# A hedgehog-attention + FFN layer on one core: the attention tiles rewritten and laid between the FFN matmuls in a fixed order

## The chip, the cores and the metric

The kernel runs on one core of a Trainium2 chip. The metric is the device time of one execution in microseconds (us), and lower is better. "Span" is the time from the first to the last instruction in the trace; the device time is about 2 us longer.

Engines are named as in the profile: PE (TensorE matmuls), PEld (PE's weight loads, which overlap its matmuls), DVE (VectorE), ACT (ScalarE), POOL (GpSimd), SP (SyncE, here a DMA queue). PSUM is the memory that PE writes to; DVE and ACT copy results out of it ("evict").

"Tile" below means 128 of the 2048 tokens, so there are 16 tiles.

## The reference

```
x: 2048 x 640, H = 32 heads of 20, F = 1728
q, k, v  = layernorm(x) @ wqkv                      # LayerNorm 1
pq, pk   = per head: q @ w_phi, k @ w_phi           # 20 x 20 each
phi_q    = [softmax(pq), softmax(-pq)]  (40 features), phi_k the same
kv, z    = sum over tokens of phi_k^T v, phi_k      # per head, needs ALL tokens
o        = (phi_q @ kv) / (phi_q . z + 1e-6)
h        = x + o @ wo
out      = h + silu(layernorm(h) @ w1) @ w2         # LayerNorm 2, FFN
```

The state kv needs every token's keys. So all keys come first (the key stage), and the queries and the FFN of a tile can follow at any time after that.

## The kernel before

It has four stages, one after another: LayerNorm 1 and folding `w_phi` into the projection weights; the key stage; the query stage for all 16 tiles; the FFN in four groups of four tiles. A tool orders the instructions of each engine. These are the parts that the change touches, with cuts marked:

```python
def p1_stage_AB(t):                       # key stage, tile t
    psv = ...; psk = ...                  # V and K projections, columns split 512 + 128
    ...
    nc.scalar.activation(Ek4[:, :, 0, 0:DH], psk3, AF.Exp, scale=1.0)
    nc.scalar.activation(Ek4[:, :, 1, 0:DH], psk3, AF.Exp, scale=-1.0)
    nc.vector.tensor_reduce(Sk[:], Ekb[:, :, 0:DH], axis=AX.X, op=ALU.add)   # L258
    nc.vector.reciprocal(Sk[:], Sk[:])                                       # L259
    nc.vector.tensor_tensor(Ekb..., Ekb..., Sk broadcast, op=ALU.mult)       # L260
...
def p2_stage_A/N(t): ...                  # query: projection, exp, and the same three
                                          # DVE operations again (L369 to L371)
def p2_stage_C1/C2(t): ...                # 16 transposes of Eq, evicted by ACT
def p2_stage_E(t): ...                    # output = numerator / denominator (DVE)
def p2_stage_G(t): ...                    # o @ wo, and x added by matmuls with the identity
def ln2_tile(t, pool): ...                # LayerNorm 2: bn_stats etc. on DVE
...
def ffn_q(q):
    for fc in range(FC):
        rows = P if fc < FC - 1 else 64   # 1728 = 13 x 128 + 64
        ...                               # first product, 5 matmuls of 512 columns
        nc.scalar.activation(sg[0:rows, :], psh[0:rows, :], AF.Sigmoid)
        nc.vector.tensor_tensor(shT[0:rows, fc, :], psh[0:rows, :], sg[0:rows, :], op=ALU.mult)
    for si in range(4):
        for n0, n1 in ((0, 512), (512, 640)):
            for fc in range(FC):
                rows = P if fc < FC - 1 else 64
                nc.tensor.matmul(psy[:, n0:n1], shT[0:rows, fc, ...], w2_sb[0:rows, fc, n0:n1], ...)
```

The softmax here doesn't subtract the row's maximum and nothing guards it: scores larger than these inputs give would overflow.

Of the kernel before, what the change touches and what calls it, by code (L numbers as in the profile page):

```python
# [10 lines left out]
AX = mybir.AxisListType  # L11

BF16 = mybir.dt.bfloat16
F32 = mybir.dt.float32


@with_exitstack
def kernel(
# [11 lines left out]
    nc = tc.nc  # L30
# [3 lines left out]
    S = T * P  # L34
# [5 lines left out]
    FC = 14  # L40
    EPS = 1e-5

    x_t = A_x.rearrange("b (t p) d -> p (b t) d", p=P)
    out_t = out.rearrange("b (t p) d -> p (b t) d", p=P)

    persist = ctx.enter_context(tc.tile_pool(name="persist", bufs=1))
    early = ctx.enter_context(ExitStack())
    lnp = early.enter_context(tc.tile_pool(name="ln1", bufs=1))
    fp_ = early.enter_context(tc.tile_pool(name="fold", bufs=1))
    fps = early.enter_context(tc.tile_pool(name="foldps", bufs=2, space=bass.MemoryType.PSUM))  # L50
    lns = early.enter_context(tc.tile_pool(name="ln1s", bufs=3))
    lnps = early.enter_context(tc.tile_pool(name="ln1ps", bufs=2, space=bass.MemoryType.PSUM))
# [3 lines left out]
    eps_t = persist.tile([P, 1], F32, name="eps_t")  # L56
    nc.gpsimd.memset(eps_t[:], EPS)
    nhalf_t = persist.tile([P, 1], F32, name="nhalf_t")
    nc.gpsimd.memset(nhalf_t[:], -0.5)

    wqkv_sb = fp_.tile([P, C, 3 * D], BF16, name="wqkv_sb")
    wqkv_v = A_wqkv.rearrange("(c p) n -> p c n", p=P)
    nc.sync.dma_start(wqkv_sb[:, :, 1 * D : 2 * D], wqkv_v[:, :, 1 * D : 2 * D])
    WPH = fp_.tile([DH, H, DH], BF16, name="WPH")
    nc.scalar.dma_start(WPH[:], A_w_phi.rearrange("h d f -> d h f"))
    X_sb = lnp.tile([P, T, D], BF16, name="X_sb")
    for g4 in range(4):
        nc.gpsimd.dma_start(
            X_sb[:, 4 * g4 : 4 * (g4 + 1), :], x_t[:, 4 * g4 : 4 * (g4 + 1), :]
        )  # L70
    for i in (2, 0):
        nc.sync.dma_start(wqkv_sb[:, :, i * D : (i + 1) * D], wqkv_v[:, :, i * D : (i + 1) * D])
    wo_sb = persist.tile([P, C, D], BF16, name="wo_sb")
    nc.sync.dma_start(wo_sb[:], A_wo.rearrange("(c p) n -> p c n", p=P))
    XT = persist.tile([P, C, S], BF16, name="XT")
    for c in range(C):
        nc.sync.dma_start_transpose(XT[:, c, :], A_x[0, :, c * P : (c + 1) * P])

    SID = fp_.tile([DH, 3 * P], BF16, name="SID")
    nc.gpsimd.memset(SID[:], 0.0)  # L80
    nc.vector.tensor_copy(SID[:, P : P + DH], ident[0:DH, 0:DH])
    phi_sb = fp_.tile([P, C, D], BF16, name="phi_sb")
    for r in range(C):
        pphi = fps.tile([P, H, 32], F32, name="psw")
        heads = []
        for h in range(H):
            r0 = DH * h
            if r0 // P != r and (r0 + DH - 1) // P != r:
                continue
            p0 = r0 - r * P  # L90
            heads.append((h, p0))
        for (h, p0) in heads:
            nc.tensor.matmul(
                pphi[:, h, 0:DH],
                SID[:, P - p0 : 2 * P - p0],
                WPH[:, h, :],
                start=True,
                stop=True,
            )
        h_lo = heads[0][0]  # L100
        h_hi = heads[-1][0] + 1
        if h_lo > 0:
            nc.gpsimd.memset(phi_sb[:, r, 0 : DH * h_lo], 0.0)
        if h_hi < H:
            nc.gpsimd.memset(phi_sb[:, r, DH * h_hi : D], 0.0)
        nc.scalar.copy(
            phi_sb[:, r, DH * h_lo : DH * h_hi].rearrange("p (h f) -> p h f", f=DH),
            pphi[:, h_lo:h_hi, 0:DH],
        )

    Wfq = persist.tile([P, C, D], BF16, name="Wfq")
    Wfk = persist.tile([P, C, D], BF16, name="Wfk")
    Wv = persist.tile([P, C, D], BF16, name="Wv")
    XnT = persist.tile([P, C, S], BF16, name="XnT")

    nc.vector.tensor_copy(Wv[:], wqkv_sb[:, :, 2 * D : 3 * D])

    WTs = {}
    for which in (1, 0):
        base = which * D  # L120
        WT = fp_.tile([P, C, D], BF16, name=f"WT{which}")
        for r in range(C):
            pwt = fps.tile([P, C, P], BF16, name="pwt")
            for ce in range(C):
                nc.tensor.transpose(  # L125
                    pwt[:, ce, :],
                    wqkv_sb[:, ce, base + r * P : base + (r + 1) * P],
                    ident[:],
                )
            nc.scalar.copy(WT[:, r, :], pwt[:].rearrange("p a b -> p (a b)"))  # L130
        WTs[which] = WT

    Xn = lnp.tile([P, T, D], BF16, name="Xn")

    def ln1_group(g):
        for tt in range(8):
            t = g * 8 + tt
            stats = lns.tile([P, 2, 6], F32, name="st1")
            for i in range(2):
                nc.vector.bn_stats(stats[:, i, :], X_sb[:, t, i * 320 : (i + 1) * 320])  # L140
            mv = lns.tile([P, 2], F32, name="mv1")
            nc.vector.bn_aggr(mv[:], stats[:])
            rstd = lns.tile([P, 1], F32, name="rstd1")
            nc.vector.tensor_scalar_add(rstd[:], mv[:, 1:2], EPS)
            nc.gpsimd.tensor_tensor(rstd[:], rstd[:], nhalf_t[:], op=ALU.pow)
            nmr = lns.tile([P, 1], F32, name="nmr1")
            nc.vector.tensor_scalar(
                out=nmr[:], in0=mv[:, 0:1], scalar1=rstd[:, 0:1], scalar2=-1.0,
                op0=ALU.mult, op1=ALU.mult,
            )  # L150
            nc.vector.tensor_scalar(
                out=Xn[:, t, :], in0=X_sb[:, t, :],
                scalar1=rstd[:, 0:1], scalar2=nmr[:, 0:1],
                op0=ALU.mult, op1=ALU.add,
            )
        for c in range(C):
            pst = lnps.tile([P, 8, P], BF16, name="pXT")
            for tt in range(8):
                t = g * 8 + tt
                nc.tensor.transpose(pst[:, tt, :], Xn[:, t, c * P : (c + 1) * P], ident[:])  # L160
            if g == 0:
                nc.vector.tensor_copy(
                    XnT[:, c, g * 8 * P : (g + 1) * 8 * P],
                    pst[:].rearrange("p a b -> p (a b)"),
                )
            else:
                nc.scalar.copy(
                    XnT[:, c, g * 8 * P : (g + 1) * 8 * P],
                    pst[:].rearrange("p a b -> p (a b)"),
                )  # L170

    def fold(which):
        Wf = Wfk if which == 1 else Wfq
        WT = WTs[which]
        for ce in range(C):
            psw = fps.tile([P, D], F32, name="psw")
            for n0, n1 in ((0, 512), (512, 640)):
                for r in range(C):
                    nc.tensor.matmul(  # L179
                        psw[:, n0:n1],  # L180
                        WT[:, r, ce * P : (ce + 1) * P],
                        phi_sb[:, r, n0:n1],
                        start=(r == 0),
                        stop=(r == C - 1),
                    )
            if which == 1:
                nc.scalar.copy(Wf[:, ce, :], psw[:])
            else:
                nc.vector.tensor_copy(Wf[:, ce, :], psw[:])  # L189

    ln1_group(0)
    fold(1)
    fold(0)
    ln1_group(1)
    early.close()

    wpool = ctx.enter_context(tc.tile_pool(name="wpool", bufs=1))
    w1_sb = wpool.tile([P, C, F], BF16, name="w1_sb")
    nc.sync.dma_start(w1_sb[:], B_w1.rearrange("(c p) n -> p c n", p=P))
    w2_sb = wpool.tile([P, FC, D], BF16, name="w2_sb")  # L200
    nc.sync.dma_start(
        w2_sb[:, 0:13, :], B_w2[0 : 13 * P].rearrange("(c p) n -> p c n", p=P)
    )
    nc.sync.dma_start(w2_sb[0:64, 13, :], B_w2[13 * P : F, :])
    HnT = wpool.tile([P, C, S], BF16, name="HnT")

    KVBD = persist.tile([P, 16, 42], BF16, name="KVBD")
    nc.vector.memset(KVBD[:], 0.0)
    p2pre_ctx = ctx.enter_context(ExitStack())
    p2pre = p2pre_ctx.enter_context(tc.tile_pool(name="p2pre", bufs=1))  # L210
    p1ctx = ctx.enter_context(ExitStack())
# [10 lines left out]
    def p1_stage_AB(t):  # L222
# [11 lines left out]
        for n0, n1 in ((0, 512), (512, 640)):  # L234
# [29 lines left out]
            op=ALU.mult,  # L264
        )
        ek_state[t] = Ek
        vp_state[t] = Vp

    def p1_stage_C(t):
        Ek = ek_state[t]  # L270
# [364 lines left out]
```

## Time and profile before

| | before |
|---|---|
| device time, median | 351.51 us (350.58 to 352.51, 4 runs) |
| span of the profiled run | 350.2 us |
| what limits, by stage | DVE from 56 to 211 us, PE from 211 us on |

These are lines of the profile page of the kernel before: busy time of each engine with its share of the span, then the shares of the chain of work that ended last, by engine.

```profile
PE 301.1 (86%) x2597; PEld 171.2 (49%) x2642; DVE 235.3 (67%) x407; ACT 164.9 (47%) x239; POOL 62.0 (18%) x101
...
PE 49%; DVE 33%; ACT 6%; DMA 4%; POOL 4%; issue 3%; SPq 0%; DVEq 0%; POOLq 0%; ACTq 0%
```

The averages say little: PE 86%, DVE 67%. The windows view of the kernel before tells more. Each row is a stretch of time, its length, the busy us of each engine in it (with the number of instructions), the clock granted to PE as a share of full speed, the DMA share and GB/s. The stretches are load and folding, key stage, query stage, FFN.

```profile
core 0: us, PE busy (x) PEld busy (x) DVE busy (x) ACT busy (x) POOL busy (x), PEclk, DMA share, GB/s
0.00:56.00 56.00, 38.85 (x320) 24.18 (x326) 39.84 (x115) 19.89 (x32) 23.01 (x48) 1.00 0.57 153
56.00:115.00 59.00, 52.27 (x577) 30.95 (x585) 54.79 (x49) 37.01 (x55) 17.32 (x26) 1.00 0.22 77
115.00:211.00 96.00, 78.10 (x958) 53.85 (x972) 86.92 (x167) 68.40 (x91) 21.11 (x26) 0.96 0.01 1
211.00:350.00 139.00, 131.84 (x746) 62.25 (x760) 53.70 (x78) 39.64 (x63) 0.55 (x1) 1.00 0.06 20
```

In the query stage DVE is busy for 86.9 of 96 us; in the FFN PE is busy for 131.8 of 139 us while DVE is busy for 53.7. Two different engines limit two stages, and in each stage the other engine has time to spare.

Next, from the timeline of the kernel before, DVE alone, a stretch of the key stage: start, duration, operation.

```profile
68.42 1.49 DVE L260 TENSOR_TENSOR Ek<-Ek,Sk 128x1280 bf16<-128x1280 bf16 x1
69.82 1.48 DVE L258 TENSOR_REDUCE Sk<-Ek 128x64 f32<-128x1280 bf16 x1
71.34 0.55 DVE L259 RECIPROCAL Sk<-Sk 128x64 f32<-128x64 f32 x1
72.00 1.49 DVE L260 TENSOR_TENSOR Ek<-Ek,Sk 128x1280 bf16<-128x1280 bf16 x1
```

From one multiply to the next is 3.58 us, with no idle time between: this stage runs at DVE's pace.

The last extract is from the timeline of the kernel before, weight loads alone, in the second FFN product.

```profile
270.61 0.09 PEld L587 LDWEIGHTS <-shT 64*128 64x128 bf16 x1 [0.42 <-issue]
270.93 3.48 PEld L587 LDWEIGHTS <-shT 128*128 128x128 bf16 x27 [0.23 <-issue]
274.83 0.09 PEld L587 LDWEIGHTS <-shT 64*128 64x128 bf16 x1 [0.42 <-issue]
275.15 3.48 PEld L587 LDWEIGHTS <-shT 128*128 128x128 bf16 x27 [0.23 <-issue]
```

The load of the 64-row chunk takes no longer than the others (0.09 us), but there is a gap before it (0.42 us) and after it (0.23 us).

### The profile page before, as it was taken

To read this page: it belongs to the slowest core of one execution; us is meant where nothing else is said; L and a number is where in the kernel's file an instruction comes from. 1 tells how busy PE (TensorE), PEld (TensorE's weight loads), DVE (VectorE), ACT (ScalarE), POOL (GpSimd) and SP (SyncE) were. 2 spreads that over 40 slices of the span, in tenths; PEclk is the share of its full clock that TensorE was granted. 3 is DMA by queue.
4 is the path that set the end of the run, shared out by engine and by line. 5 is a ranking of instruction groups with operands and counts; after the bars stand their busy time and mean duration, and the time that the engine had idled before them with its cause. 6 is when DMAs were issued, how large, how long until landed. Compare 5 with 4: busy or idle time off the path is not lost.

```text
span 350.2 us, 6321 instructions
## 1 busy us (share of the span) xinstructions
PE 301.1 (86%) x2597; PEld 171.2 (49%) x2642; DVE 235.3 (67%) x407; ACT 164.9 (47%) x239; POOL 62.0 (18%) x101
## 2 busy tenths in 40 slices
PE   2299878999996779788999667999999999999995
PEld 2156445555553556455665543445544544444443
DVE  0985987999999999998989865441453145315421
ACT  3253049646466567867899455420742044104400
POOL 7430552333320012342231010000000000000000
PEclk9999999999999989999999899999999999999999
DMA  7995003910000000000000000001000100010011
GB/s 274 400 196 108 2 1 83 392 35 2 2 0 2 3 0 2 2 0 2 3 2 1 2 0 2 0 20 38 19 2 19 39 19 1 21 38 18 2 37 37
DMA packets 18997, 15.98 MB, mean 46 GB/s; under 512 B 11482, under 2 KB 17818, under 8 KB 18970
## 3 DMA queue, kind: packets, MB, share of 16 engines
q1 hardware_dynamic: 17744, 12.95, 12.8%
q0 software_dynamic: 576, 2.62, 1.8%
q8 instruction: 20, 0.33, 0.4%
q10 hardware_dynamic: 650, 0.03, 0.1%
q14 instruction: 7, 0.06, 0.0%
HBM read 10.35 MB, written 2.62 MB: 37 GB/s over the span
## 4 chain that ended last, share of the span: by engine, by line
PE 49%; DVE 33%; ACT 6%; DMA 4%; POOL 4%; issue 3%; SPq 0%; DVEq 0%; POOLq 0%; ACTq 0%
PE psy L587 19%; PE psh L569 16%; DVE Ek L260 6%; DVE Sk L258 6%; DMA wqkv_sb<-in_A_wqkv_dram 4%; PE psw L179 4%; DVE Sq L369 4%; PE psa L442 3%; DVE O L419 2%; DVE Sk L259 2%; DVE Eq L371 2%; DVE st L485 2%; POOL rstd L490 2%; PE psq L349 2%; PE psT L395 1%
## 5 line engine op out<-in xcount | busy, mean ns | idle before, releaser
L587 PE MATMUL psy<-w_sb,shT 128*128 128x128 bf16 (+3 forms) x441 | 72.4, 299 | 0.7 <-issue 0.5
L569 PE MATMUL psh<-HnT,w_sb 128*128 128x512 bf16 (+1 forms) x272 | 66.7, 379 | 2.9 <-DVE shT L578 1.7
L578 DVE TENSOR_TENSOR shT<-psh,sg 128x512 bf16<-128x512 f32 (+1 forms) x56 | 38.6, 691 | 38.3 <-ACT sg L577 38.3
L577 ACT ACTIVATE sg<-psh 128x512 bf16<-128x512 f32 (+1 forms) x56 | 33.3, 596 | 65.7 <-PE psh L569 61.4
L587 PEld LDWEIGHTS <-shT 128*128 128x128 bf16 (+1 forms) x448 | 33.7, 97 | 35.2 <-issue 10.4
L569 PEld LDWEIGHTS <-w_sb 128*128 128x128 bf16 (+1 forms) x280 | 26.7, 98 | 36.3 <-issue 8.4
L595 DVE TENSOR_TENSOR o_t<-psy,H_sb 128x640 bf16<-128x640 f32 x16 | 13.2, 824 | 43.4 <-PE psy L587 43.4
L442 PE MATMUL psa<-wo_sb,OT 128*128 128x512 bf16 (+1 forms) x150 | 27.1, 308 | 1.4 <-ACT OT L434 0.5
L236 PE MATMUL p1mm<-Wfk,XnT 128*128 128x128 bf16 (+1 forms) x152 | 25.3, 294 | 1.6 <-ACT Ek L256 0.4
L226 PE MATMUL p1mm<-Wv,XnT 128*128 128x128 bf16 (+1 forms) x159 | 24.9, 299 | 1.1 <-DVE Wfq L189 1.0
L349 PE MATMUL psq<-Wfq,XnT 128*128 128x128 bf16 (+1 forms) x134 | 23.6, 295 | 2.3 <-ACT Eq L362 1.7
L258 DVE TENSOR_REDUCE Sk<-Ek 128x64 f32<-128x1280 bf16 x16 | 23.6, 1476 | 2.4 <-ACT Ek L256 2.4
L260 DVE TENSOR_TENSOR Ek<-Ek,Sk 128x1280 bf16<-128x1280 bf16 x16 | 23.7, 1483 | 1.4
L388 ACT COPY EqT<-psT 128x1024 bf16<-128x1024 bf16 x16 | 16.3, 1018 | 12.4 <-PE psT L387 12.3
L255 ACT ACTIVATE Ek<-p1mm 128x640 bf16<-128x640 f32 x16 | 11.3, 703 | 20.5 <-PE p1mm L236 17.2
L371 DVE TENSOR_TENSOR Eq<-Eq,Sq 128x1280 bf16<-128x1280 bf16 x14 | 20.8, 1483 | 0.1
L369 DVE TENSOR_REDUCE Sq<-Eq 128x64 f32<-128x1280 bf16 x14 | 20.5, 1474 | 0.0
L359 POOL MEMSET Eq<- 128x768 bf16 x14 | 10.3, 743 | 55.7 <-PE psT L395 50.2
L490 POOL TENSOR_TENSOR rstd<-rstd,nhalf_t 128x1 f32<-128x1 f32 x16 | 13.5, 845 | 34.9 <-DVE rstd L489 34.7
L398 ACT COPY EqT<-psT 128x1024 bf16<-128x1024 bf16 x16 | 16.3, 1016 | 6.9 <-PE psT L395 6.8
L140 DVE BATCH_NORM_STATS2 st<-X_sb 128x6 f32<-128x320 bf16 x32 | 14.2, 463 | 7.8 <-DMA X_sb<-in_A_x_dram 7.8
L125 PE MATMUL pwt<-ident,wqkv_sb 128*128 128x128 bf16 x50 | 6.7, 307 | 13.2 <-DMA wqkv_sb<-in_A_wqkv_dram 6.8
(91 smaller groups left out, 457.9 us busy)
## 6 DMA issues: line engine op xcount, KB each, us to landing
X_sb<-in_A_x_dram POOLq DMA_DIRECT2D x4, 640.0 KB, 9.1
out_dram<-o_t SPq DMA_DIRECT2D x16, 160.0 KB, 1.8
wqkv_sb<-in_A_wqkv_dram SPq DMA_DIRECT2D x3, 800.0 KB, 11.3
w_sb<-in_B_w_dram SPq DMA_DIRECT2D x1, 2160.0 KB, 8.1
w_sb<-in_B_w_dram SPq DMA_DIRECT2D x1, 2080.0 KB, 13.9
wo_sb<-in_A_wo_dram SPq DMA_DIRECT2D x1, 800.0 KB, 16.2
XT<-in_A_x_dram SPq DMA_TRANSPOSE x5, 5.8
w_sb<-in_B_w_dram SPq DMA_DIRECT2D x1, 80.0 KB, 12.8
```

Of the source, the lines that this page charges most:

```text
L226: nc.tensor.matmul(psv[:, n0:n1], XnT[:, c, t * P : (t + 1) * P], Wv[:, c, n0:n1], start=(c == 0), stop=(c == C - 1),)
L236: nc.tensor.matmul(psk[:, n0:n1], XnT[:, c, t * P : (t + 1) * P], Wfk[:, c, n0:n1], start=(c == 0), stop=(c == C - 1),)
L258: nc.vector.tensor_reduce(Sk[:], Ekb[:, :, 0:DH], axis=AX.X, op=ALU.add)
L260: nc.vector.tensor_tensor(Ekb[:, :, 0:DH], Ekb[:, :, 0:DH], Sk[:].unsqueeze(2).to_broadcast([P, 64, DH]), op=ALU.mult,)
L349: nc.tensor.matmul(psq[:, n0:n1], XnT[:, c, t * P : (t + 1) * P], Wfq[:, c, n0:n1], start=(c == 0), stop=(c == C - 1),)
L369: nc.vector.tensor_reduce(Sq[:], Eqb[:, :, 0:DH], axis=AX.X, op=ALU.add)
L371: nc.vector.tensor_tensor(Eqb[:, :, 0:DH], Eqb[:, :, 0:DH], Sq[:].unsqueeze(2).to_broadcast([P, 64, DH]), op=ALU.mult,)
L442: nc.tensor.matmul(psa[:, n0:n1], OT[:, c, :], wo_sb[:, c, n0:n1], start=(c == 0), stop=False,)
L569: nc.tensor.matmul(psh[0:rows, :], w1_sb[:, c, fc * P : fc * P + rows], HnT[:, c, q * 512 : (q + 1) * 512], start=(c == 0), stop=(c == C - 1),
L577: nc.scalar.activation(sg[0:rows, :], psh[0:rows, :], AF.Sigmoid)
L578: nc.vector.tensor_tensor(shT[0:rows, fc, :], psh[0:rows, :], sg[0:rows, :], op=ALU.mult)
L587: nc.tensor.matmul(psy[:, n0:n1], shT[0:rows, fc, si * P : (si + 1) * P], w2_sb[0:rows, fc, n0:n1], start=(fc == 0), stop=(fc == FC - 1),)
```

## The change

The kernel was written anew. Its intent: take work off DVE and PE, and put each group's attention tiles between the FFN matmuls of the group before, so that DVE's work for attention runs under PE's work for the FFN. PE's order is now the order of the source text. The core of it, with cuts marked:

```diff
-        for n0, n1 in ((0, 512), (512, 640)):        # all projections, and the second FFN product
+        for half in range(2):                         # 320 + 320 columns
...
-        # query: exp, reduce, reciprocal, multiply, 16 transposes
+    def stageQ(g, r, ps):                             # features computed already transposed
+        for c in range(C):
+            nc.tensor.matmul(ps, Wfq[:, c, r * P : (r + 1) * P], XnT[g][:, c, :], ...)
+        for s in range(2):
+            nc.scalar.activation(EqT[g][:, s, r, :], ps, AF.Exp, scale=1.0 - 2.0 * s)
+    def stageD(t):                                    # products with the state, for +s and -s,
+        ...                                           # each with the sum of its features (column 21)
+        nc.vector.reciprocal(w[:], A[:, 1, :, :, 21])
+        nc.vector.tensor_tensor(w[:], w[:], A[:, 0, :, :, 21], op=ALU.mult)
+        for a in range(2):
+            nc.vector.tensor_tensor(u[:, a], A[:, 1, a, :, 0:21], w broadcast, op=ALU.mult)
+        nc.vector.tensor_tensor(u[:], u[:], A[:, 0, :, :, 0:21], op=ALU.add)
+        nc.vector.reciprocal(rd[:], u[:, :, :, 20])
+        nc.vector.tensor_tensor(o..., u[:, :, :, 0:DH]..., rd broadcast, op=ALU.mult)
...
+    def stageG(t):                                    # o @ wo; x added by DVE, sum as by-product
+        nc.vector.scalar_tensor_tensor(out=Xv, in0=ps[:, :, 0:320], scalar=1.0, in1=Xv, ...,
+            accum_out=st[:, 0:1])
+        nc.scalar.activation(sq[:], X[:, t, :], AF.Square, accum_out=st[:, 1:2])
+        ...                                           # five small POOL operations, then normalise (DVE)
...
-                nc.scalar.activation(sg[0:rows, :], psh[0:rows, :], AF.Sigmoid)
-                nc.vector.tensor_tensor(shT[0:rows, fc, :], psh[0:rows, :], sg[0:rows, :], op=ALU.mult)
+            nc.scalar.activation(shT[g][:, 2 * k : 2 * k + 2, :], ps[:], AF.Silu)
...
-                rows = P if fc < FC - 1 else 64
+    nc.gpsimd.memset(w1[:, :, F : FC * P], 0.0)       # last chunk padded to 128 rows
+    nc.gpsimd.memset(w2[64:128, 13, :], 0.0)
...
+        for _ in range(80):                           # warm-up matmuls while the first tile loads
+            nc.tensor.matmul(wps[:, 0, 0:P], ident[:], ident[:], start=True, stop=True)
...
+        for t in range(T):                            # key stage, in PE's order
+            stageV(t + 3); xT(t + 4); stageC(t - 2)   # V, X transposes, key-value product
+            if 6 <= t <= 10: early_q.pop(0)()         # a piece of the query weights' folding
+            stageK(t)
+            if t >= 1 and not 6 <= t <= 10 and early_q: early_q.pop(0)()
...
+        for g in range(G):                            # FFN steps of group g, with the tiles of
+            ...                                       # group g + 1 between them
+                plan = [(0, stageT, b), (0, stageD, b + 1), (1, stageG, b), ...]
```

`mm`, the pool that nearly every PE stage writes to, has two PSUM buffers of two banks.

## The prediction

> **What bounds the kernel now.** By the windows view it runs in stages. 0–56 us: load, LayerNorm 1, folding. 56–115 us: key stage; DVE is over 95% busy and the chain of waits is mostly DVE: reduce 1.476, reciprocal 0.55, multiply 1.483 us, a 3.58 us step per tile. 115–213 us: query stage, again DVE about 95% (the same three operations, plus 0.35 + 0.80 us for the output division and about 2 us of LayerNorm 2), 5.5–6 us per tile, with PE stalls. 213–350 us: FFN, PE 96–99% busy, little on DVE and ACT. So the two limits alternate.
>
> **What the change does.**
> 1. Query normalisation goes: two halves are combined by a ratio w of their denominators. Removed: reduce + reciprocal + multiply, 3.5 us x 16 = 56 us of DVE. Added: six operations on the PSUM result; from the 640-wide (0.80–0.82 us) and 512-wide (0.69) PSUM operations I estimate 0.35+0.2+2x0.5+0.85+0.35+0.8 = 3.55 us per tile. No gain.
> 2. Query features are computed transposed: 256 transposes (56 ns each in the timeline, 14 us of PE) and 32.6 us of ACT evictions go. DVE adds the residual, not 80 matmuls (4.5 us of PE).
> 3. LayerNorm 2 statistics come from the accumulator outputs of the residual add and of an ACT square: about 2 us per tile on DVE becomes 1.0 + 0.44.
> 4. Sigmoid + multiply becomes one Silu: 38.6 us of DVE and 33.3 of ACT become 29 of ACT. "ScalarE: Activation LUTs" (What ACT_TABLE_LOAD costs) gives about 1283 ns per load; the trace shows two of 1283; the build again has two.
> 5. Columns are split 320+320, not 512+128, and the 64-row last FFN chunk is padded. Now F2 takes 147 ns per matmul (78 in 11.5 us) against 136 by columns: about 5 us.
> 6. Attention tiles of the next group are interleaved into the FFN of this one: the main gain.
>
> **Sum.** PE columns: 625,872 to 595,616, of which 10,240 are warm-up dummies during the load. "TensorE: Matmul & The Clock Gate" (Part 1) gives N/2.4 GHz + 2.5 ns; the timeline agrees (10 of 512 columns in 2.16 us). That is about 249 us of useful PE work, the floor.
>
> Start: four tiles of LayerNorm run in turn through POOL, about 2.3 us each; V, transposes and folding last to about 24 us. In the instruction order all 16 tiles' statistics precede the first key reduce on DVE: it starts near 30 us. Keys stay DVE-bound: 16 x 3.58 + 2 = 59 us, end near 90; last key matmuls and masking: first query product at 93.5. Left on PE: 177 us (55 attention, 122 FFN). Stalls: 6 before the FFN (DVE 5.0 us per tile against PE 4.9), 5 within. Tail 3.5.
> 93.5 + 177 + 11 + 3.5 = 285 us, plus 1 outside the span: **286 us**, 272 to 302. Chances: faster 0.97, same 0.02, slower 0.01.
>
> **Right if:** PE busy 88–95%; DVE falls from 235 to about 178 us; key stage still 3.6 us per tile with DVE over 90%; FFN with attention about 41–44 us per group; F2 near 136 ns per matmul.
>
> **Wrong if:** PE, in order with two PSUM buffers, stalls more on evictions in the interleaved groups (each 1 us per tile costs 12); combine operations longer than estimated; key stage limited by PE or ACT (60 and 53 us of work in about 65); key reduces overlapping the statistics (down to 272).

## The result, and the profile after

The changed kernel takes 290.9 us (median of 11 runs, 289.1 to 292.21) against 351.27 us (16 runs of the kernel before, on the same chips). The ratio is 0.8266, 95% interval 0.8243 to 0.8289: faster. Ratios here are the mean time of one kernel's runs over the mean of the other's in the same rounds, so they are not quite the ratios of the medians. Executions over 1.5% slower than the fastest of the same kernel are left out of the means. The prediction was 286 us, range 272 to 302.

First the same two lines of the page, for the changed kernel.

```profile
PE 262.0 (91%) x2137; PEld 176.0 (61%) x2154; DVE 167.2 (58%) x292; ACT 138.5 (48%) x218; POOL 36.9 (13%) x133
...
PE 70%; DVE 15%; ACT 7%; POOL 3%; issue 2%; DMA 1%; ACTq 0%; DVEq 0%
```

PE's part of the chain that ended last rose from 49% to 70%, DVE's fell from 33% to 15%. PE's busy share is not a good gauge of how much is left: the Trainium skill, "Perfetto Trace Analysis" (Identifying the Most-Contended Engine), says so, because matmuls are pipelined, and this trace shows it. A 320-column matmul is recorded with 299 ns, but 28 in a row take 3.80 us, 136 ns each. PEld, one of the two measures that the page recommends instead, rose from 49% to 61%.

Now the windows view of the changed kernel: load and folding; key stage until the first attention product; the tiles before the FFN; FFN with the other twelve attention tiles between.

```profile
0.00:30.00 30.00, 21.99 (x230) 17.73 (x231) 18.98 (x58) 15.38 (x24) 12.74 (x51) 1.00 0.97 345
30.00:98.00 68.00, 62.62 (x596) 45.66 (x596) 59.95 (x59) 48.41 (x80) 1.39 (x2) 1.00 0.01 2
98.00:130.00 32.00, 24.60 (x201) 15.27 (x206) 21.92 (x48) 20.05 (x39) 7.11 (x20) 1.00 0.00 1
130.00:288.00 158.00, 152.83 (x1112) 97.34 (x1121) 66.34 (x129) 54.67 (x78) 15.68 (x60) 1.00 0.05 18
```

The last row carries all of the FFN and 12 of 16 attention tiles in 158 us; the FFN alone took 139 us before. DVE is less than half busy there, so its attention work is hidden.

The waits view of the changed kernel, PE alone, says where PE still stands still. It gives who waited for whom: us in total, times, longest. First from 98 to 130 us:

```profile
PE mm L387 <- ACT EqT L265: 1.4, 1, 1.4
PE mm L387 <- DVE o L376: 1.3, 2, 1.0
PE mm L387 <- ACT HnT L432: 1.1, 1, 1.1
PE psD L354 <- DVE KVBD L248: 1.0, 1, 1.0
PE mm L261 <- ACT EqT L265: 0.9, 1, 0.9
PE mm L396 <- ACT ot L389: 0.8, 1, 0.8
```

The same view from 130 us to the end has one line, 1.5 us. That wait ends when the first FFN matmul starts, at 130.19 us, so it still belongs to the stretch before the FFN. Inside the FFN the list has no wait of PE at all.

```profile
PE mm L457 <- ACT HnT L432: 1.5, 1, 1.5
```

And the timeline of the changed kernel, PE alone, in the key stage. L202 are the K and V projections, L235 the key-value product, L157 the X transposes, L171 the query weights' transposes.

```profile
43.24 0.44 PE L157 MATMUL q<-ident,xn 128*128 128x128 bf16 x5 [0.38 <-ACT wT L172]
43.52 0.83 PE L235 MATMUL kv<-Vp,Ek 128*128 128x168 bf16 x12
44.21 1.52 PE L202 MATMUL mm<-Wfk,XnT 128*128 128x320 bf16 x10
45.56 0.44 PE L171 MATMUL q<-ident,wq 128*128 128x128 bf16 x5
45.84 1.52 PE L202 MATMUL mm<-wv,XnT 128*128 128x320 bf16 x10
47.75 0.44 PE L157 MATMUL q<-ident,xn 128*128 128x128 bf16 x5 [0.38 <-ACT wT L172]
```

From 43.24 to 47.75 is 4.5 us for one key tile, about 4.0 of them PE work (without the marked wait for a copy, the tile takes 3.96 us in the run c_after_k below). I had predicted 3.58 us, DVE's pace. This is the main reason why the first attention product came 4.7 us later than my sum said.

Term by term, from the trace of the profiled run:

| term | predicted | measured |
|---|---|---|
| first attention product starts at | 93.5 us | 98.2 us |
| from there to the first FFN matmul | about 29 us (23 of work, 6 of waits) | 32.0 us (25 and 7.0) |
| FFN with twelve tiles | about 159 us (154 of work, 5 of waits) | 153.7 us (no waits) |
| tail (last eviction and store) | 3.5 us | 3.8 us |
| span | about 285 us | 287.7 us |

Where the 62.5 us between the two profiled spans (350.2 and 287.7 us) were won can be read from the timelines. The first attention product starts at 98.2 instead of 116.3 us, which is 18 us. All of that is a shorter start: from the first key reduce on DVE (48.7 us before, 30.7 us after) to that product both kernels take about 67.5 us. From there to the first FFN matmul at 211.2 us the kernel before needs 94.8 us for the attention of 16 tiles; the changed one needs 32.0 us for four tiles and about 32 us of PE inside the FFN for twelve, which is about 30 us less (each kernel also does some query projections in its key stage). The FFN itself takes 139 us before and about 125 us without the attention tiles in it (the run serial2 below), which is 14 us less. My list of changes has no point for the shorter start, though my sum had it in ("near 30 us"). No run took it apart: loads, LayerNorm and folding all changed there, and x is read in another token layout.

One thing about reading the times. The runs of the changed kernel lie on a ladder: 289.1 to 289.6 us where the recorded clock of the core is 1.000, 290.9 to 291.1 at 0.994, 292.1 and 292.2 at 0.988. The traces of two other kernels that were profiled at 0.994 (no_warm and split512 below) show what such a step is. In each, the recorded clock is 1.00 up to the tail except for one spell of about 3.4 us at 0.50, among PE's waits before the FFN (122.4 to 125.8 us in no_warm). One such spell costs about 1.5 us (290.9 against 289.4 us). That 0.988 stands for two spells fits, but no run at 0.988 was profiled. So where two kernels differ by 1 or 2 us, I also compare runs of equal recorded clock.

### The profile page after: what moved, and what is told of

Its sections match the earlier page's. It is cut to its first block, busy times and chain, and to the rows that moved or that the text cites. A ratio compares the mean times of both kernels' runs of the same rounds, so it can differ in the third digit from the quotient of the medians.

```text
span 287.7 us, 5118 instructions
## 1 busy us (share of the span) xinstructions
PE 262.0 (91%) x2137; PEld 176.0 (61%) x2154; DVE 167.2 (58%) x292; ACT 138.5 (48%) x218; POOL 36.9 (13%) x133
## 3 DMA queue, kind: packets, MB, share of 16 engines
q1 hardware_dynamic: 7920, 12.62, 12.3%
## 4 chain that ended last, share of the span: by engine, by line
PE 70%; DVE 15%; ACT 7%; POOL 3%; issue 2%; DMA 1%; ACTq 0%; DVEq 0%
PE mm L471 21%; PE mm L457 21%; PE mm L202 9%; PE mm L396 7%; DVE stats L138 4%; PE kv L235 3%; PE psD L354 3%; DVE Ek L227 3%; ACT Ek L219 2%; DVE Sk L225 2%; PE mm L261 2%; DVE xn L145 2%; POOL rstd L142 2%; DMA X<-in_A_x_dram 1%; PE q L157 1%
## 5 line engine op out<-in xcount | busy, mean ns | idle before, releaser
L457 PE MATMUL mm<-HnT,w 128*128 128x512 bf16 x270 | 62.5, 379 | 2.4 <-ACT HnT L432 1.5
L471 PE MATMUL mm<-w,shT 128*128 128x320 bf16 x448 | 63.8, 299 | 0.0
L471 PEld LDWEIGHTS <-shT 128*128 128x128 bf16 x448 | 43.1, 98 | 16.4
L457 PEld LDWEIGHTS <-w 128*128 128x128 bf16 x280 | 27.1, 98 | 32.2 <-issue 2.2
L461 ACT ACTIVATE shT<-mm 128x1024 bf16<-128x1024 f32 x28 | 28.6, 1023 | 35.5 <-PE mm L457 35.5
L202 PEld LDWEIGHTS <-XnT 128*128 128x128 bf16 x320 | 29.8, 98 | 15.2 <-ACT XnT L158 4.8
L219 ACT ACTIVATE Ek<-mm 128x640 bf16<-128x640 f32 x32 | 20.8, 701 | 17.9 <-PE mm L202 12.7
L202 PE MATMUL mm<-wv,XnT 128*128 128x320 bf16 x160 | 24.4, 300 | 4.1 <-ACT XnT L158 4.1
L396 PE MATMUL mm<-wo,ot 128*128 128x320 bf16 x160 | 24.4, 299 | 0.8 <-ACT ot L389 0.8
L227 DVE TENSOR_TENSOR Ek<-Ek,Sk 128x1280 bf16<-128x1280 bf16 x16 | 23.9, 1492 | 1.2
L202 PE MATMUL mm<-Wfk,XnT 128*128 128x320 bf16 x160 | 24.3, 299 | 0.0
L396 PEld LDWEIGHTS <-ot 128*128 128x128 bf16 x160 | 15.6, 98 | 8.4 <-ACT ot L389 1.0
```

Of the source, the lines that this page charges most:

```text
L202: nc.tensor.matmul(ps[:, half, 0:320], xT_of(t)[:, c, :], W[:, c, half * 320 : (half + 1) * 320], start=(c == 0), stop=(c == C - 1),)
L219: nc.scalar.activation(Ek[:, s, :].rearrange("p (a n) -> p a n", a=2), ps[:, :, 0:320], AF.Exp, scale=1.0 - 2.0 * s,)
L227: nc.vector.tensor_tensor(Ek3, Ek3, Sk[:].unsqueeze(2).to_broadcast([P, 2 * H, DH]), op=ALU.mult)
L396: nc.tensor.matmul(ps[:, half, 0:320], ot_of[t][:, c, :], wo[:, c, half * 320 : (half + 1) * 320], start=(c == 0), stop=(c == C - 1),)
L457: nc.tensor.matmul(ps[:, i, :], w1[:, c, fc * P : (fc + 1) * P], HnT[g][:, c, :], start=(c == 0), stop=(c == C - 1),)
L461: nc.scalar.activation(shT[g][:, 2 * k : 2 * k + 2, :], ps[:], AF.Silu)
```

## The experiments

Twelve kernels were run. Each edit is against the changed kernel unless it says otherwise.

### 1. Is the overlap the main gain? (serial, serial2)

The first edit does all attention before the FFN:

```diff
         fill(20)
+        stageT(4)
+        for t in range(4, T):
+            if t > 4: stageTHT(t - 1, t)
+            if t + 1 < T: stageD(t + 1)
+            stageG(t)
+        stageTH(T - 1)
...
-            if g + 1 < G:        # the tiles of group g + 1 between the FFN steps
+            if False:
```

(All four groups' normalised, transposed inputs must now be kept, so they take over the buffers of the first LayerNorm's.)

> The changed kernel with the same instructions, but the attention tiles 4 to 15 all done before the first FFN group instead of between its matmuls. Theory (overlap is the main gain): alone, an attention tile costs what DVE needs, about 4.9 us (3.5 for the combine, 0.9 residual, 0.45 normalise), or more through the round trips; inside the FFN it costs only its 2.7 us of PE. So 12 x (4.9 to 6) instead of 12 x 2.7: 26 to 40 us slower, 317 to 330 us. Rival (the gain is the work taken away from PE, order matters little): within 8 us of the changed kernel, under 299 us.

Measured: 365.84 us (4 runs), 75 us slower, even slower than the kernel before. The direction was right, the size was missed by a factor of two. The windows view of this run, over the twelve tiles:

```profile
130.00:238.00 108.00, 58.29 (x401) 41.53 (x399) 53.01 (x114) 27.06 (x51) 21.90 (x60) 0.69 0.00 1
```

DVE is busy for only 53 of 108 us, so it was not DVE's work that cost 9 us per tile. My order let each tile wait for the normalised output of the tile before, and PE's granted clock fell to 0.69. So this run tells the price of a bad serial order, not of missing overlap. The second edit skews the tiles against each other:

```diff
+        for t in range(4, T):
+            if t + 1 < T: stageD(t + 1)
+            stageT(t)
+            stageG(t)
+            if t >= 6: stageTH(t - 2)
+        stageTH(T - 2); stageTH(T - 1)
```

(The normalised inputs lie where they do in serial, and the LayerNorm 2 output has four buffers instead of two.)

> As the serial run (all attention before the FFN), but with the tiles pipelined against each other: the attention product of tile t+1 goes before the transposes of tile t, and the LayerNorm transposes two tiles late, so that no step waits for the one just before it. Theory (the 75 us of the serial run were not DVE's work but the chain of one tile through PE, DVE, ACT, POOL, about 8.9 us, with PE idle enough that its granted clock fell to 0.7): a tile now costs DVE's 4.9 us or a little more, 5.0 to 6.0, at a granted clock back over 0.9: 12 x (5.0 to 6.0) in place of 12 x 2.7, 318 to 331 us. Rival (DVE or the round trips cost 8 us or more however the tiles are ordered): over 350 us.

Measured: 328.01 us (4 runs), 37 us slower than the changed kernel, inside the expected range.

```profile
130.00:193.00 63.00, 41.32 (x371) 29.76 (x369) 48.03 (x110) 23.73 (x44) 17.13 (x52) 0.86 0.00 1
```

This view shows most of the twelve tiles, with DVE the busiest engine (48 of 63 us). By the timeline they last from 130.4 us to the first FFN matmul at 201.2 us: 71 us, 5.9 us each. Inside the FFN they cost 2.7 us each: 153.7 us less the FFN's 121.4 us (an estimate from 280 matmuls at 216 ns and 448 at 136 ns), over 12. That difference of 38.5 us is all of the 38.7 us between the spans of the two profiled runs; the FFN of this run took no longer (about 121 us from its first to its last matmul). So the overlap is worth about 37 us of the 60 in this kernel, against the best serial order that I tried. It is not worth the 75 us of the first try. Even this order left DVE idle: it was busy for 50 of the 71 us, and PE's granted clock was 0.86. A serial order at DVE's full pace, which I did not find, would make the overlap worth about 18 us (an estimate: 38.7 less the 21 us of idling).

### 2. Does DVE's work in the FFN count? (sigmoid, bn_stats2)

```diff
-            nc.scalar.activation(shT[g][:, 2 * k : 2 * k + 2, :], ps[:], AF.Silu)
+            sg = work.tile([P, 2, 512], BF16, name="sg", bufs=2)
+            nc.scalar.activation(sg[:], ps[:], AF.Sigmoid)
+            nc.vector.tensor_tensor(shT[g][:, 2 * k : 2 * k + 2, :], ps[:], sg[:], op=ALU.mult)
```

(To make room for the new buffer, this run too keeps the normalised inputs in the first LayerNorm's buffers.)

> The changed kernel with Sigmoid on ACT and the product on DVE (28 of 1024 columns from PSUM, about 1.2 us each, 34 us of DVE) in place of Silu. Theory (FFN is bound by PE and DVE is only half busy there, but PE has just two PSUM buffers, which are held 1.2 us longer): a wait wherever a short stage stands between two first-FFN units, about 1 us each, 9 to 18 us slower in all, 300 to 309 us. Rival A (DVE has room, nothing waits): under 293 us. Rival B (DVE work counts in full): 34 us slower, 325 us.

Measured: 308.77 us, 17.9 us slower. DVE's busy time from 130 us on rose from 66 to 99 us, by 33 us, and stayed well below the length of the stage (174 us); about half of the 33 came through as time. The waits view of this run, PE alone, in the FFN:

```profile
PE mm L456 <- DVE shT L462: 7.3, 9, 1.5
PE mm L439 <- DVE shT L462: 2.7, 6, 0.8
PE mm L456 <- ACT ot L388: 2.1, 3, 0.7
PE mm L472 <- ACT ot L446: 2.0, 3, 0.7
PE mm L456 <- ACT ot L446: 2.0, 3, 0.7
```

With these five lines PE waits for 16 us, where the changed kernel waited for none of them. A PSUM buffer is held until the product is done, there are two of them, and wherever a short stage (transposes, L439, or the next unit after them, L456) follows, PE comes back for a buffer too early. So Silu is worth 18 us here by freeing PSUM sooner, as the waits show, not by the 38.6 us of DVE that it removes. (A run with a third PSUM buffer would test that directly; there is none.)

The second edit puts DVE work back in another place, the LayerNorm 2 statistics:

```diff
-            nc.vector.scalar_tensor_tensor(out=Xv, ..., accum_out=st[:, 0:1])
-            nc.scalar.activation(sq[:], X[:, t, :], AF.Square, accum_out=st[:, 1:2])
-            ...                              # five POOL operations
+            nc.vector.tensor_tensor(Xv, ps[:, :, 0:320], Xv, op=ALU.add)
+            for k in range(2):
+                nc.vector.bn_stats(st[:, k, :], X[:, t, k * 320 : (k + 1) * 320])
+            nc.vector.bn_aggr(m[:], st[:])
+            ...                              # two POOL operations
```

> The changed kernel with the LayerNorm 2 statistics computed as before, by two statistics instructions and an aggregate on DVE from the stored sum, instead of the accumulator outputs of the residual add and of an ACT square followed by five small POOL operations (two remain). It puts 1.0 to 1.1 us of DVE per tile back (17 us in all) and takes 0.9 us of ACT and 0.7 us of POOL away. Theory (in the FFN the DVE is half idle and PE does not wait, so 12 of the 16 tiles are free; in the 32 us before the FFN, DVE and the round trips count, so four tiles cost up to 1.1 us each, less what the shorter chain through ACT and POOL gives back): 0 to 4 us slower, 290 to 295 us. Rival (the point of the prediction that lists it as a saving of about 0.6 us per tile counts in full): 9 us or more slower, over 299 us.

Measured: 291.25 us (5 runs), ratio 0.8287 to the kernel before, where the changed kernel has 0.8266. At equal recorded clock it is 1.8 us slower (291.2 against 289.4 us). DVE's busy time rose by 15.6 us (167.2 to 182.8) while ACT's fell by 12.6 and POOL's by 10, and the time moved by under 2 us: off the limiting path DVE's work cost nearly nothing, as this theory said and my own list of savings did not make clear.

### 3. The 64-row chunk or the 512 + 128 split? (rows64, split512, before_pad)

My point 5 took both together. The first edit uses 64 rows again in the second FFN product:

```diff
+                rows = P if fc < FC - 1 else 64
...
-                    ps[:, half, 0:320], shT[g][:, fc, i * P : (i + 1) * P],
-                    w2[:, fc, half * 320 : (half + 1) * 320],
+                    ps[:, half, 0:320], shT[g][0:rows, fc, i * P : (i + 1) * P],
+                    w2[0:rows, fc, half * 320 : (half + 1) * 320],
```

> The changed kernel, but the last chunk of the second FFN product is again read with 64 rows instead of 128 padded ones (32 of the 448 matmuls). Theory (the 64-row chunk breaks the overlap of weight load and matmul, about 0.15 us each as the weight-load gaps before it show): 32 x 0.15 = 5 us slower, 295 to 296 us. Rival (the 147 ns per matmul of before come from the 512+128 columns): no difference, within 1 us.

Measured: 296.84 us; at recorded clocks of 0.998 and 1.0, 295.3 and 295.4 against 289.4 us, so 5.9 us slower. Over 32 such matmuls that is 0.19 us each. The weight loads show it (timeline, weight loads alone): first the changed kernel, then two lines of this run.

```profile
154.97 3.77 PEld L471 LDWEIGHTS <-shT 128*128 128x128 bf16 x28
...
155.16 1.73 PEld L472 LDWEIGHTS <-shT 128*128 128x128 bf16 x13
157.16 0.90 PEld L472 LDWEIGHTS <-shT 64*128 64x128 bf16 x7 [0.26 <-issue]
```

Where the changed kernel loads 28 weights in a row, a gap stands before the one with 64 rows. The Trainium skill, "TensorE: Matmul & The Clock Gate" (Part 2, Step-by-step), says that the number of rows does not matter for the time of a weight load. The load itself agrees (in the kernel before, 0.093 us on average with 64 rows and 0.098 us with 128), but the matmuls around it do not follow each other as closely.

The second edit splits the second FFN product into 512 + 128 columns again:

```diff
+                n0, n1 = ((0, 512), (512, 640))[half]
-                    ps[:, half, 0:320], ..., w2[:, fc, half * 320 : (half + 1) * 320],
+                    ps[:, half, 0 : n1 - n0], ..., w2[:, fc, n0:n1],
...                                                  # the final add reads the 640 columns in one piece
```

> The changed kernel, but the second FFN product is again split into 512 and 128 columns instead of 320 and 320. Theory (the split costs nothing by itself: bursts of ten in the key stage of before took 1.36 us with either split, and the 147 ns came from the 64-row chunk): within 1 us of the changed kernel, 290 to 292 us. Rival (my prediction's wording, the split is a part of the 5 us; weight loads of about 98 ns do not hide behind 128-column matmuls of 56 ns): 2 to 10 us slower.

Measured: 293.41 us; at recorded clock 1.0, 292.5 against 289.4 us, 3.1 us slower. Neither theory said why. In the timeline a whole tile of the product, 28 matmuls, takes 3.81 us as with 320 + 320, so the split by itself costs nothing. The waits view of this run has the reason (PE alone, FFN):

```profile
PE mm L396 <- ACT ot L447: 1.8, 3, 0.6
...
PE mm L472 <- DVE X L402: 0.6, 3, 0.2
```

The half tile of 128 columns lasts only 0.78 us, and in one place of the plan it is what stands between the transposes and the output projection that needs their copies. Equal halves cover that wait, unequal ones do not. These two lines make 2.4 of the 3.1 us; the rest stays open.

The third edit pads the kernel before:

```diff
-    w1_sb = wpool.tile([P, C, F], BF16, name="w1_sb")
+    w1_sb = wpool.tile([P, C, FC * P], BF16, name="w1_sb")
+    nc.gpsimd.memset(w1_sb[:, :, F : FC * P], 0.0)
+    nc.gpsimd.memset(w2_sb[64:128, 13, :], 0.0)
-                rows = P if fc < FC - 1 else 64         # in both FFN products
+                rows = P
```

> The kernel before with its last FFN chunk padded to 128 rows of zeros and nothing else changed. Theory (64-row chunk costs 0.31 us per tile of the second product): 16 x 0.31 = 5 us faster, about 346 us, and the second product at 136 ns per matmul. Rival (512+128 columns are the cause): no gain, 351 us, 147 ns per matmul.

Measured: 350.25 us, ratio 0.9982, 95% interval 0.9957 to 1.0008: the expected 5 us did not come. From the traces, the time from the first FFN matmul to the end fell from 139.0 us (211.16 to 350.2) to 132.0 us (215.63 to 347.6), so the FFN did gain 7 us. But the first FFN matmul came 4.5 us later. With the edit, the ordering tool also arranged the work before the FFN differently (DVE waits 6.6 us before its key reduce at 55 us, where the kernel before has no wait of that length), so this run changed two things, and it is not a clean test. My guess is that the two POOL memsets did it; no run shows it. The clean one is rows64, in a kernel whose PE order is fixed.

### 4. What limits the key stage? (no_key_norm, c_after_k, fold_first, no_warm)

```diff
-        nc.vector.tensor_reduce(Sk[:], Ek3, axis=AX.X, op=ALU.add)
-        nc.vector.reciprocal(Sk[:], Sk[:])
-        nc.vector.tensor_tensor(Ek3, Ek3, Sk[:]..., op=ALU.mult)
```

> The changed kernel without the reduce, reciprocal and multiply on the keys (3.5 us of DVE per tile, 56 us in all); the result is wrong on purpose. Theory (the first ten key tiles are bound by PE in its fixed order, 4.0 to 4.5 us each; DVE binds only the start and the last tiles): key stage ends 6 to 12 us earlier, 279 to 285 us. Rival (the prediction: DVE binds all key tiles): two to three of the three operations' time is saved per tile beyond PE's mean 3.7, over 20 us, under 271 us.

Measured: 286.25 us; at recorded clock 1.0, 3.3 us faster than the changed kernel. The first attention product came at 94.8 instead of 98.2 us. Taking 56 us of work away from DVE gained 3 us. The windows view of this run from 30 to 95 us:

```profile
30.00:95.00 65.00, 62.03 (x601) 46.11 (x602) 4.63 (x10) 48.69 (x80) 1.39 (x2) 1.00 0.01 2
```

DVE has 4.6 us of work in 65 us, and the stage is hardly shorter: a tile still takes 4.5 us on PE (41.77 to 46.28 us in the timeline, 0.40 of it a wait for one of ACT's copies). PE and its waits for copies limit the stage. The gain is even less than the theory expected. (The kernel leaves a step of the reference out, and this is no valid kernel.)

```diff
-            if t >= 2: stageC(t - 2)
             if 6 <= t <= 10: early_q.pop(0)()
             stageK(t)
+            if t >= 2: stageC(t - 2)
```

> The changed kernel with the key-value product of tile t-2 placed after the key projection of tile t instead of before it. Theory (PE binds the middle of the key stage, and 0.33 to 0.38 us per tile of tiles 1 to 5 is a wait for the copy out of the one shared PSUM bank that weight transposes and X transposes use; the new order gives that copy 0.7 us more): five waits gone, 1.5 to 2.5 us faster, 288.5 to 289.5 us. Rival (DVE binds): no change, within 0.5 us of 290.9.

Measured: 286.83 us (4 runs, all at recorded clock 1.0), 2.6 us faster than the changed kernel at equal clock. PE in the same part of the key stage (timeline):

```profile
40.84 0.44 PE L157 MATMUL q<-ident,xn 128*128 128x128 bf16 x5
41.12 1.52 PE L202 MATMUL mm<-Wfk,XnT 128*128 128x320 bf16 x10
42.48 0.83 PE L235 MATMUL kv<-Vp,Ek 128*128 128x168 bf16 x12
43.17 0.44 PE L171 MATMUL q<-ident,wq 128*128 128x128 bf16 x5
43.45 1.52 PE L202 MATMUL mm<-wv,XnT 128*128 128x320 bf16 x10
44.80 0.39 PE L157 MATMUL q<-ident,xn 128*128 128x128 bf16 x4
```

One tile now takes 3.96 us (40.84 to 44.80) instead of 4.5, and the 0.38 us wait is gone. The product of an older tile is the right thing to put where a copy needs time. No work was removed, and the stage got shorter, which it could not have done had DVE limited it throughout.

The next edit was to start the keys earlier:

```diff
+        phb mask product first on DVE, before the LayerNorm of tile 0
-        for t in range(3): xT(t); stageV(t)
-        for r in range(C): wT(1, r)
-        for ce in range(C): fold(1, ce)
+        xT(0); wT(1, 0); wT(1, 1); xT(1); wT(1, 2); wT(1, 3); wT(1, 4); xT(2); fold(1, 0) ... fold(1, 4)
...
-            stageV(t + 3)          # before the X transposes of tile t + 4
+            stageV(t)              # after stageK(t)
```

> The changed kernel with the key weights transposed and folded before any V projection (the mask product first on DVE, V of tile t made beside K of tile t instead of three tiles ahead). Theory (the key stage starts late, first reduce at 30.7 us, because folding stands behind three V tiles, and V three tiles ahead overloads PE in the middle while DVE waits 7 us in total): first key exponentials near 20 us instead of 27.9, key stage ends 5 to 9 us earlier, 282 to 286 us. Rival (DVE's own work, LayerNorm and keys, is the limit from the start): under 2 us gained.

Measured: 303.23 us, 12.3 us slower, at recorded clocks of 0.96 to 0.97. The timeline shows two mistakes of mine. On DVE, which works in order, the mask product waited until 8.7 us for its small weights to arrive, and all of LayerNorm waited behind it: the first statistics began at 9.65 instead of 4.96 us. And X transposes now follow the query weights' transposes directly, which share one PSUM bank: PE waits 1.1 us for each copy. The waits also slowed PE (timeline, PE alone):

```profile
25.03 0.72 PE L157 MATMUL q<-ident,xn 128*128 128x128 bf16 x5 [3.20 <-DVE xn L145]
25.54 2.87 PE L202 MATMUL mm<-Wfk,XnT 128*128 128x320 bf16 x10
28.21 2.87 PE L202 MATMUL mm<-wv,XnT 128*128 128x320 bf16 x10
```

After 3.2 us of idling, ten matmuls take 2.67 us (25.54 to 28.21) instead of 1.36. The Trainium skill, "TensorE: Matmul & The Clock Gate" (Part 1), describes that: PE falls to half its clock after about 3.4 us of idling and needs as long to come back. The trace agrees on the half clock but not quite on the times: here 3.2 us of idling were enough, and the matmuls stayed slow for about 5.8 us (25.03 to 30.87). So this run says nothing about how early the keys could start, only that this order does not do it.

```diff
-        for _ in range(80):        # warm-up matmuls
+        for _ in range(1):
```

> The changed kernel with one warm-up matmul instead of 80. Theory (the 80 run while PE waits for the first tile, but they keep the granted clock at 1.0 for what follows, and PE, with gaps of over 1 us per V tile until 24 us, would not be granted it soon): 2 to 10 us slower, a clock under 0.8 in some slices before 40 us. Rival (my sum: they cost and gain nothing, the start is bound by LayerNorm on DVE and POOL and by ACT copies): within 1 us of 290.9.

Measured: 291.58 us (median of 6 runs; one of them, 293.72 us, is marked slow and left out of the ratio), ratio 0.829, where the changed kernel has 0.8266: no difference beyond noise, and the two kernels' fastest runs, both at recorded clock 1.0, are 289.3 and 289.1 us. The rival, my sum, was right. The first V tile did run cold: its ten matmuls took 2.64 us instead of 1.37. The start is so full of waits for LayerNorm and copies that the 1.3 us were absorbed.

### 5. A faster version (best)

```diff
-        for t in range(3): xT(t); stageV(t)
-        for r in range(C): wT(1, r)
+        xT(0); stageV(0); xT(1); wT(1, 0); stageV(1); wT(1, 1); xT(2); wT(1, 2); stageV(2); wT(1, 3); wT(1, 4)
...
+            # key-value product before stageK only where a fold is (6 <= t <= 10), else after it
...
         stageTH(3)
         fill(20)
+        stageT(4)                  # out of the plan of FFN group 0
+        stageD(5)
```

> The changed kernel with three moves in PE's order: the key-value product after the key projection in the tiles without a fold, the key weights' transposes put into the gaps between the first V tiles, and the transposes of tile 4 and the attention product of tile 5 put ahead of the first FFN unit, which waits 1.5 us for a copy. Theory (PE's order is the limit from 25 us on): 2.6 us (as the run that moved the product alone, at equal clock) + 1 for the fold tiles' five waits of 0.19 + 1 to 1.5 earlier start + 1: 283.5 to 285.5 us. Rival (DVE takes over as soon as PE is faster in the key stage): 286 to 288 us, no better than that run.

Measured: 284.79 us (5 runs, 284.64 to 286.1), ratio 0.8111 (95% interval 0.809 to 0.8132). It is correct, and beats both kernels: 4.6 us faster than the changed kernel at equal recorded clock. The first attention product came at 94.2 us. Its remaining waits of PE, 28 to 96 us:

```profile
PE kv L235 <- DVE Ek L227: 2.3, 2, 1.7
PE psD L362 <- DVE KVBD L248: 1.0, 1, 1.0
PE q L157 <- ACT wT L172: 0.3, 1, 0.3
```

The wait for the query weights' copies (L157 on L172) fell from 1.8 to 0.3 us. The wait for DVE's key normalisation (L227) hardly changed (2.3 us; 2.5 in the changed kernel) and is now most of what is left, so the next step in this stage would probably have to come from DVE as well. Between 94 and 126 us the same round trips remain as before (7.5 us), except that tile 4's transposes took the place of the wait in front of the FFN.

## Why the prediction was right, and where its steps were wrong

The time fell within the range (290.9 in 272 to 302), 1.7% above the stated 286. The mechanism was the predicted one; that the number came so close is partly luck, because errors of up to 5 us in the terms cancelled.

- **What bounds the kernel.** Right: the query stage was DVE's, the FFN PE's, and joining them was the main gain. serial2 puts it at 37 of the 60 us, against the best serial order tried. Another 18 us came from the shorter start, which my list of changes did not name.
- **Point 1, no gain on DVE from the combine.** Right, and the sizes held: 0.355 + 0.187 + 2 x 0.502 + 0.854 + 0.353 + 0.824 = 3.58 us per tile against 3.55 estimated. The Trainium skill, "VectorE: DVE Perf Modes" (its errata section), gives (N + 151) / 0.96 ns for a two-tensor fp32 add. For 672 columns the estimate from it is 857 ns; the trace has 854, and my scaling had said 850.
- **Points 3 and 4, less work on DVE.** The work went: DVE fell from 235 to 167 us (178 forecast; I did not trace the other 11). But the prediction did not say what it is worth. bn_stats2 shows that DVE work inside the FFN is worth almost nothing, and sigmoid shows that its place, holding a PSUM buffer, is worth much. The count of two table loads of 1283 ns held too.
- **Point 2, fewer transposes and no residual matmuls.** No run took this back, so what it is worth alone stays open.
- **Point 5, columns and padding, "about 5 us".** The 5 us are there (5.9 by rows64, 136 ns per matmul as forecast), but they belong to the 64 rows. Going back to the 512 + 128 split costs 3 us, mostly by leaving a wait uncovered.
- **The key stage: "Keys stay DVE-bound: 16 x 3.58 + 2 = 59 us, end near 90".** This step failed. DVE did start where I said (30.68 us), but ended at 95.2: 64.5 us, of which it waited 5.4 us for ACT's key exponentials. DVE set the pace in tiles 0 to 2 and again near the end. In tiles 3 to 10 it was PE with its waits for copies: 4.5 us per tile with a query-weight transpose and 4.0 with a fold, not 3.6, and DVE was busy for 88% of the stage, not over 90%. no_key_norm took all of DVE's key work away and gained 3.3 us. I had listed "key stage limited by PE" among what could go wrong, with 60 us of PE work in 65, and still took DVE's sum. In a fixed order 60 of 65 is no slack: the V projections run three tiles ahead, so PE's work is bunched into the first tiles, while DVE has time to spare there and binds only at the start and the end.
- **The waits.** Before the FFN I said 6 us; 7.0 us stand in the two lists of waits (without the 1.0 us before the first attention product, with the 1.5 us before the first FFN matmul), and the stretch is 3 us longer than forecast. In the FFN I allowed 5 us, and PE waited for nothing. This error had the opposite sign to the 4.7 us of the key stage and these 3 us, so the total was closer than its parts.
- **The time outside the span** was 1.7 us rather than 1 in the profiled run, and the lower recorded clock of 6 of the 11 runs brought the median from 289.4 to 290.9 us.

What stays open: how early the key stage can start (fold_first was no fair test of it), what each part of the shorter start is worth, and why a spell of half clock comes in some runs and not in others.

## What to carry to other kernels

When two stages have different limits and the data allow it, put the one's work between the other's; here an attention tile inside the FFN then cost what it needs of PE (2.7 us), where alone it cost 5.9 us. In a fixed order with few PSUM buffers, what matters of an operation is how long it holds a buffer and what stands between it and the next use. Sum each engine per tile where the order bunches its work, not over the whole stage, and test "which engine limits" by taking that engine's work away.

## What the Trainium skill lacked or had wrong

- "TensorE: Matmul & The Clock Gate" says that the row count does not matter for a weight load. It lacks that a 64-row chunk among 128-row ones breaks the close sequence: 0.19 us for each such matmul (5.9 us for 32), though the load itself stays at 0.09 us. "TensorEngine Tiling" (Key Properties) says that changing the tiling mode drains PE, but gives no time for it; whether a 64-row chunk is such a change, no run shows.
- "TensorE: Matmul & The Clock Gate" describes the half clock well (ten 320-column matmuls: 2.67 us after 3.2 us of idling, 1.36 us warm), though the slow spell lasted about 5.8 us in fold_first, longer than the 3.4 us that it gives. It warns that the trace's clock records can be unreliable. Here too: in no_warm the records give 1.00 for the first 20 us, while the first V tile took 2.64 us.
- No page that I read says what reading an accumulator costs: 0.08 us on DVE and 0.19 us on ACT for each, seen in the trace as an instruction of its own.
